# Token layout and a masked multiply for the first chunk's four attention tiles

## The chip, the core and the metric

The kernel runs on one core of one Trainium2 chip. The metric is device time in microseconds (us), the median of several runs. The engines work side by side, each through its own queue in order: PE (TensorE: matmuls and transposes, results in PSUM), DVE (VectorE) and ACT (ScalarE), which do elementwise work, POOL (GpSimd), which does elementwise work on SBUF alone, and SP (SyncE), which only issues transfers here.

## What is computed

A linear attention with a decaying state over 768 tokens (4 batches, 8 heads of 48 channels), then two feed-forward blocks on its 3072 token rows of 384 channels. The attention, cut to what the change touches:

```
for t in range(S):
    cur = einsum('bhd,bhe->bhde', u * k[t], v[t])
    y[t] = einsum('bhd,bhde->bhe', r[t], state + cur)
    state = w[t][..., None] * state + einsum('bhd,bhe->bhde', k[t], v[t])
x = y.transpose(0, 2, 1, 3).reshape(B * S, H * D)
h = x @ moe_w_in;  g = h * clip(h + 3, 0, 6) / 6;  x = g @ moe_w_out
```

The second block (`moe2`) comes after that and is not touched.

## The kernel before

**Tiles and stages.** The tokens are cut into 6 chunks of 128; with 4 batches that makes 24 tiles, tile i being chunk i // 4 of batch i % 4. The attention of a tile goes through six stages. `stw` clips the decay w (`wc`, L403). `st0` transposes w and r on PE (`wt`, `rt`, L397), and DVE runs a cumulative product over the tokens from each side (`q` at L427, `e` at L433, in four instructions each) and scales r by it (L437). `st1` transposes k (`kt`), DVE scales it (`q`, L452), and POOL forms z = r * k * u (L454, L455). `st2` transposes the scaled k back to tokens (`ktp`, copied to `ktok` by ACT) and forms the products of all keys and queries: `pa0` for the even and `pa1` for the odd heads (L477), 128 x 4 x 128 each. DVE sums z to a diagonal d (L473); POOL writes ident * d into `am` (L483), and DVE copies pa over it where the causal mask is set (L487). `st3` computes the state update `kv` (L497), copied into `s_st` by DVE (L523), and the output `yt` (L511) with **channels on the partitions**: v is the weight (48 columns) and `am` the moving operand (128 columns). ACT copies it out (`ys`, L527), two transfers write it to `x1d` in DRAM (L528), and one reads it back as `xf`, with 384 channels as three groups of 128 partitions (L530). `st4` splits it into a high part `xh` (ACT, L546) and a low part `xl` (POOL, L547).

**The first feed-forward block** runs in slots: `ffn_in(n)` is nine matmuls over `xh` and `xl` with the high and low parts of the weights (`h`, L565), then ACT, DVE, ACT and DVE or POOL (`t`, `gh`, `gl`, L569 to L573); `ffn_out(n)` follows two slots later (`y`, L585). One chunk (four tiles) takes 16 slots. It starts when `xh` and `xl` of tiles 0 to 3 are there.

**The weights** of the first block come as 64-bit floats in 16 blocks and are decoded on the way: per block four DVE steps on 128x768 (L40, L43, L50, L53), an ACT copy for the high part (`w_h`, L60) and a POOL subtraction for the low part (`w_l`, L61). Blocks 0 to 3 are begun ahead of the slots, the others at one per slot.

**What sets the order.** Ahead of the slots, a table of ticks calls the stages of tiles 0 to 3 (`starts` and `decodes`, L677 to L690). In it SP and POOL keep the order in which the code issues their work, while a scheduler orders PE, DVE and ACT. Attention tiles share three PSUM buffers (`ps_tile`, L391), so a stage's PE work waits until an earlier tile's PSUM has been read. From tile 4 on the scheduler spreads the stages over the slots.

Of the kernel before, what the change touches and what calls it, by code (L numbers as in the profile page):

```python
# [8 lines left out]
F32 = mybir.dt.float32  # L9
# [3 lines left out]
ACTF = mybir.ActivationFunctionType  # L13
# [5 lines left out]
P = 128  # L19
# [248 lines left out]
def fast_path(  # L268
# [189 lines left out]
    def st2(i):  # L458
        a = at[i]
        g = i // B  # L460
        kq = a["q"][:, :, 1:C + 1]
        rr = a["e"]
        if g < NG - 1:
            ktp = ps_tile("ktp")
            for hp in range(HP):
                nc.tensor.transpose(out=ktp[:, hp, 0:DP], in_=kq[0:DP, hp, :], identity=ident[0:DP, 0:DP])
            ktok = atp.tile([P, HP, DP], F32, tag="ktok", name="ktok")
            nc.scalar.activation(out=ktok, in_=ktp[:, :, 0:DP], func=ACTF.Copy)
            a["ktok"] = ktok
        a["am"] = []  # L470
        pas = [ps_tile("pa0"), ps_tile("pa1")]
        d = atp.tile([P, H], F32, tag="d", name="d")
        nc.vector.tensor_reduce(out=d, in_=a["z"], axis=AX.X, op=ALU.add)  # L473
        heads = [(j, hh) for j in range(HP) for hh in range(2)]
        for j, hh in heads:
            pa, o = pas[hh], 64 * hh
            nc.tensor.matmul(  # L477
                out=pa[:, j, :], lhsT=kq[o:o + D, j, :], rhs=rr[o:o + D, j, :], start=True, stop=True
            )
        dv = d.rearrange("p (j hh) -> p hh j", hh=2)  # L480
        for hh, pa in enumerate(pas):
            am = atp.tile([P, 4, C], F32, tag="am", name="am")
            nc.gpsimd.tensor_tensor(  # L483
                out=am, in0=ident.unsqueeze(1).to_broadcast([P, HP, C]),
                in1=dv[:, hh, :].unsqueeze(2).to_broadcast([P, HP, C]), op=ALU.mult,
            )
            nc.vector.copy_predicated(am, causal.unsqueeze(1).to_broadcast([P, HP, C]), pa)  # L487
            a["am"].append(am)

    def st3(i):  # L490
        a = at[i]
        g, b = divmod(i, B)
        vv = a["v"].rearrange("p h d -> p (h d)")
        if g < NG - 1:
            kv = ps_tile("kv")
            for hp in range(HP):
                nc.tensor.matmul(  # L497
                    out=kv[0:DP, hp, 0:2 * D], lhsT=a["ktok"][:, hp, :], rhs=vv[:, hp * 2 * D:(hp + 1) * 2 * D],
                    start=True, stop=True,
                )  # L500
        y = ps_tile("yt")
        for hp in range(HP):
            for j in range(2):
                if g > 0:
                    nc.tensor.matmul(  # L505
                        out=y[64 * j:64 * j + D, hp, :], lhsT=a["sp"][0:DP, hp, j * D:(j + 1) * D],
                        rhs=a["e"][0:DP, hp, :], start=True, stop=False,
                    )
            for j in range(2):
                h = 2 * hp + j  # L510
                nc.tensor.matmul(  # L511
                    out=y[64 * j:64 * j + D, hp, :], lhsT=vv[:, h * D:(h + 1) * D], rhs=a["am"][j][:, hp, :],
                    start=(g == 0), stop=True,
                )
        if g < NG - 1:
            for j in range(2):
                o, f = 64 * j, D * j
                dst = s_st[b][o:o + D, :, f:f + D]
                src = kv[o:o + D, :, f:f + D]
                if g > 0:  # L520
                    nc.vector.tensor_tensor(out=dst, in0=src, in1=a["sp"][o:o + D, :, f:f + D], op=ALU.add)
                else:
                    nc.vector.tensor_copy(out=dst, in_=src)  # L523
        ys = atp.tile([P, HP, C], F32, tag="ys", name="ys", bufs=1)
        for j in range(2):
            o = 64 * j
            nc.scalar.activation(out=ys[o:o + D], in_=y[o:o + D], func=ACTF.Copy)  # L527
            nc.sync.dma_start(out=x1d[i, :, j].rearrange("h d t -> d h t"), in_=ys[o:o + D])  # L528
        xf = atp.tile([P, KD, C], F32, tag="xf", name="xf")
        nc.sync.dma_start(  # L530
            out=xf, in_=x1d[i].rearrange("h j d t -> (h j d) t").rearrange("(c p) t -> p c t", p=P)
        )
        a["xf"] = xf

    def st4(i):
        a = at.pop(i)
        g, b = divmod(i, B)
        if b == 0:
            x_t[g] = (
                xp.tile([P, KD, GT], F32R, tag="xh", name="xh"),  # L540
                xp.tile([P, KD, GT], F32R, tag="xl", name="xl"),
            )
        xh, xl = x_t[g]
        xf = a["xf"]
        sl = slice(b * C, (b + 1) * C)
        nc.scalar.activation(out=xh[:, :, sl], in_=xf, func=ACTF.Copy, accum_out=chk[:, 3 * i + 2:3 * i + 3])  # L546
        nc.gpsimd.tensor_tensor(out=xl[:, :, sl], in0=xf, in1=xh[:, :, sl].bitcast(F32), op=ALU.subtract)  # L547

    stages = [stw, st0, st1, st2, st3, st4]

# [293 lines left out]
```

## Time and profile before

| what | us |
|---|---|
| median of 3 runs (845.01 to 847.47) | 845.86 |
| the profiled execution's own time | 846.06 |
| span of its records, first to last instruction | 844.3 |
| busy in that span: PE / DVE / ACT / POOL | 784.8 / 537.1 / 350.9 / 289.6 |

The program has three parts that can be told apart in the page's slices of 21 us: up to about 84 us the attention of the first four tiles (PE 5 and 4 tenths busy in the first two slices), then the first feed-forward block until somewhat after 600 us, with the decoding of its weights up to about 174 us, and the second block behind it. A busy share is to be read by part: a mean over the span says nothing of which engine sets the pace in one of them.

### The profile page before, as it was taken

To read this page: it belongs to the slowest core of one execution; us is meant where nothing else is said; L and a number is where in the kernel's file an instruction comes from. 1 tells how busy PE (TensorE), PEld (TensorE's weight loads), DVE (VectorE), ACT (ScalarE), POOL (GpSimd) and SP (SyncE) were. 2 spreads that over 40 slices of the span, in tenths; PEclk is the share of its full clock that TensorE was granted. 3 is DMA by queue.
4 is the path that set the end of the run, shared out by engine and by line. 5 is a ranking of instruction groups with operands and counts; after the bars stand their busy time and mean duration, and the time that the engine had idled before them with its cause. 6 is when DMAs were issued, how large, how long until landed. Compare 5 with 4: busy or idle time off the path is not lost.

```text
span 844.3 us, 12276 instructions
## 1 busy us (share of the span) xinstructions
PE 784.8 (93%) x4546; PEld 661.8 (78%) x4546; DVE 537.1 (64%) x992; ACT 350.9 (42%) x655; POOL 289.6 (34%) x383
## 2 busy tenths in 40 slices
PE   5486988799999999999999999998999999999995
PEld 4364766588888888888888888786789999999995
DVE  5876999975656555555666665689564555555451
ACT  2342545444333434443444333455353443444341
POOL 4276567554333332233333321133122222222210
PEclk9766998899999999999999999999999999999998
DMA  9758354524222322232222200443011111111101
GB/s 189 138 85 205 103 181 110 121 57 123 66 57 56 85 48 57 53 83 53 57 48 52 76 19 19 115 126 113 0 66 47 39 47 48 38 47 37 39 19 34
DMA packets 149382, 62.45 MB, mean 74 GB/s; under 512 B 103872, under 2 KB 143936, under 8 KB 149312
## 3 DMA queue, kind: packets, MB, share of 16 engines
q1 hardware_dynamic: 146720, 56.84, 27.9%
q10 hardware_dynamic: 2592, 4.72, 1.5%
q8 instruction: 38, 0.62, 0.3%
q14 instruction: 32, 0.26, 0.1%
HBM read 47.39 MB, written 14.16 MB: 73 GB/s over the span
## 4 chain that ended last, share of the span: by engine, by line
PE 74%; DVE 13%; issue 5%; DMA 2%; ACT 2%; POOL 2%; SPq 1%; POOLq 0%; ACTq 0%; DVEq 0%
PE y L585 18%; PE h L565 17%; PE po L780 12%; PE h L753 12%; DVE dec L50 3%; PE pa L477 3%; PE yt L511 3%; PE pt L767 2%; PE yt L505 2%; DVE dec L53 2%; PE kv L497 2%; DVE raw L43 1%; DVE dec L40 1%; DVE t L570 1%; PE wt L397 1%
## 5 line engine op out<-in xcount | busy, mean ns | idle before, releaser
L569 ACT ACTIVATE t<-h,three 128x512 f32<-128x512 f32 x96 | 65.7, 684 | 134.7 <-PE h L565 134.4
L585 PE MATMUL y<-gh,w_h 128*128 128x512 f32 x288 | 121.0, 420 | 0.0
L565 PE MATMUL h<-xh,w_h 128*128 128x512 f32 x288 | 114.3, 397 | 5.5 <-DVE t L570 5.5
L565 PE MATMUL h<-xl,w_h 128*128 128x512 f32 x288 | 113.3, 393 | 3.7 <-POOL xl L547 3.7
L585 PE MATMUL y<-gh,w_l 128*128 128x512 f32 x288 | 113.5, 394 | 0.0
L565 PE MATMUL h<-xh,w_l 128*128 128x512 f32 x288 | 113.4, 394 | 0.0
L585 PE MATMUL y<-gl,w_h 128*128 128x512 f32 x288 | 113.3, 394 | 0.0
L571 ACT ACTIVATE gh<-t 128x512 fp32r<-128x512 f32 x96 | 60.5, 630 | 85.9 <-DVE t L570 85.7
L570 DVE SCALAR_TENSOR_TENSOR t<-t,h 128x512 f32<-128x512 f32 x96 | 65.4, 681 | 45.1 <-ACT t L569 45.1
L483 POOL TENSOR_TENSOR am<-ident,d 128x512 f32<-128x512 f32 x48 | 54.3, 1149 | 109.7 <-PE yt L511 109.5
L573 DVE TENSOR_TENSOR gl<-t,gh 128x512 fp32r<-128x512 f32 x88 | 71.7, 815 | 29.3 <-ACT gh L571 27.8
L427 DVE TENSOR_TENSOR_SCAN q<-wt,ones 112x128 f32<-112x128 f32 x96 | 34.5, 407 | 69.2 <-PE wt L397 69.2
L565 PEld LDWEIGHTS h<-xh,w_h 128*128 128x128 f32 x288 | 54.7, 190 | 19.7 <-DVE t L570 8.5
L67 DVE TENSOR_REDUCE nm<-h 128x1 f32<-128x1024 f32 x24 | 29.4, 1225 | 62.5 <-PE h L753 62.5
L780 PE MATMUL po<-w_oh,qh 128*128 128x384 f32 x192 | 67.0, 349 | 0.3 <-ACT qh L769 0.3
L565 PEld LDWEIGHTS h<-xl,w_h 128*128 128x128 f32 x288 | 54.7, 190 | 15.7 <-POOL xl L547 4.5
L585 PEld LDWEIGHTS y<-gh,w_h 128*128 128x128 f32 x288 | 54.6, 190 | 15.5 <-issue 4.0
L780 PE MATMUL po<-w_oh,ql 128*128 128x384 f32 x192 | 65.2, 339 | 0.1
L780 PE MATMUL po<-w_ol,qh 128*128 128x384 f32 x192 | 65.0, 339 | 0.0
L585 PEld LDWEIGHTS y<-gh,w_l 128*128 128x128 f32 x288 | 54.5, 189 | 12.2
L565 PEld LDWEIGHTS h<-xh,w_l 128*128 128x128 f32 x288 | 54.6, 190 | 11.6
L585 PEld LDWEIGHTS y<-gl,w_h 128*128 128x128 f32 x288 | 54.9, 190 | 9.8 <-DVE gl L573 0.3
(104 smaller groups left out, 1616.1 us busy)
## 6 DMA issues: line engine op xcount, KB each, us to landing
raw<-in_moe_w_in_dram SPq DMA_DIRECT2D x24, 384.0 KB, 3.7
raw<-in_moe_w_out_dram SPq DMA_DIRECT2D x24, 384.0 KB, 4.2
w<-in_w_dram SPq DMA_DIRECT2D x24, 192.0 KB, 3.3
r<-in_r_dram SPq DMA_DIRECT2D x24, 192.0 KB, 3.3
k<-in_k_dram SPq DMA_DIRECT2D x24, 192.0 KB, 3.9
v<-in_v_dram SPq DMA_DIRECT2D x24, 192.0 KB, 3.0
x1d<-ys SPq DMA_DIRECT2D x48, 96.0 KB, 2.3
xf<-x1d SPq DMA_DIRECT2D x24, 192.0 KB, 2.7
```

What stands on the lines that cost most here:

```text
L50: nc.vector.scalar_tensor_tensor(out=f, in0=f, scalar=3, in1=raw[:, :, 1], op0=ALU.logical_shift_left, op1=ALU.bitwise_or)
L67: nc.vector.tensor_reduce(out=nm, in_=h, axis=AX.X, op=ALU.max, negate=True)
L427: nc.vector.tensor_tensor_scan(out=q[0:DP, hp, 0:C][:, ::-1], data0=wt[0:DP, hp, :][:, ::-1], data1=ones[0:DP, :], initial=1.0, op0=ALU.mu ...
L483: nc.gpsimd.tensor_tensor(out=am, in0=ident.unsqueeze(1).to_broadcast([P, HP, C]), in1=dv[:, hh, :].unsqueeze(2).to_broadcast([P, HP, C]), ...
L565: nc.tensor.matmul(out=h, lhsT=a, rhs=b, start=(j == 0), stop=(j == len(ops) - 1))
L569: nc.scalar.activation(out=t, in_=h, func=ACTF.Relu, bias=three)
L570: nc.vector.scalar_tensor_tensor(out=t, in0=t, scalar=6.0, in1=h, op0=ALU.min, op1=ALU.mult)
L571: nc.scalar.activation(out=gh, in_=t, func=ACTF.Copy)
L573: eng.tensor_tensor(out=gl, in0=t, in1=gh.bitcast(F32), op=ALU.subtract)
L585: nc.tensor.matmul(out=y_ps[g][c], lhsT=a, rhs=b, start=(m == 0 and j == 0), stop=(m == M1 - 1 and j == 2))
L753: nc.tensor.matmul(out=h[:, fs], lhsT=a[:, c, :], rhs=b_[:, c, fs], start=(j == 0), stop=(j == len(ops) - 1))
L780: nc.tensor.matmul(out=po, lhsT=x[:, m, :], rhs=y[:, m, :], start=(n == 0), stop=(n == 3 * M2 - 1))
```

## The change

For tiles 0 to 3 (`first`, g == 0), which have no earlier state to add:

- The products of the even heads are computed ahead of those of the odd ones. ACT copies `pa0` to `am`, and POOL masks it in place (`affine_select`, 128x512); DVE multiplies `pa1` with the mask. No diagonal is written into `am`: d * v is computed on POOL (`av`, 128x384).
- The output matmul has `am` as its weight (128 columns) and v as its moving operand (48 columns), so that **tokens** lie on the partitions. DVE adds `av` while it takes the result out of PSUM (`ys`, 128x384).
- No transfer through `x1d`: three PE transposes put `ys` into PSUM (`px`), ACT takes `xh` from there, and DVE, no longer POOL, forms `xl`.

```diff
@@ st2
+        if first:
+            heads.sort(key=lambda x: x[1])
...
+            if first:
+                if hh == 0:
+                    nc.scalar.activation(out=am, in_=pa, func=ACTF.Copy)
+                    nc.gpsimd.affine_select(
+                        out=am, in_=am, pattern=[[0, 4], [1, P]], compare_op=ALU.is_gt, fill=0.0, base=0,
+                        channel_multiplier=-1,
+                    )
+                else:
+                    mask = causal.bitcast(F32).unsqueeze(1).to_broadcast([P, 4, C])
+                    nc.vector.tensor_tensor(out=am, in0=pa, in1=mask, op=ALU.mult)
+                continue
...
+        if first:
+            d = atp.tile([P, H], F32, tag="d", name="d")
+            nc.vector.tensor_reduce(out=d, in_=a["z"], axis=AX.X, op=ALU.add)
+            av = atp.tile([P, H, D], F32, tag="xf", name="av")
+            nc.gpsimd.tensor_tensor(out=av, in0=a["v"], in1=d.unsqueeze(2).to_broadcast([P, H, D]), op=ALU.mult)
+            a["av"] = av
@@ st3
+            if g == 0:
+                for j in range(2):
+                    h = 2 * hp + j
+                    nc.tensor.matmul(
+                        out=yf[:, h * D:(h + 1) * D], lhsT=a["am"][j][:, hp, :], rhs=vv[:, h * D:(h + 1) * D],
+                        start=True, stop=True,
+                    )
+                continue
...
+        if g == 0:
+            ys = ys.rearrange("p h t -> p (h t)")[:, 0:DM]
+            nc.vector.tensor_tensor(out=ys, in0=yf, in1=a["av"].rearrange("p h d -> p (h d)"), op=ALU.add)
+            a["ys"] = ys
+            return
@@ st4
+        if g == 0:
+            xf = ps_tile("px")[:, 0:KD, :]
+            for c in range(KD):
+                nc.tensor.transpose(out=xf[:, c, :], in_=a["ys"][:, c * P:(c + 1) * P], identity=ident)
+            eng = nc.vector
+        else:
+            xf, eng = a["xf"], nc.gpsimd
...
-        nc.gpsimd.tensor_tensor(out=xl[:, :, sl], in0=xf, in1=xh[:, :, sl].bitcast(F32), op=ALU.subtract)
+        eng.tensor_tensor(out=xl[:, :, sl], in0=xf, in1=xh[:, :, sl].bitcast(F32), op=ALU.subtract)
```

The scheduler and the queues answer with another order. Three places of it follow; line numbers are those of each kernel. First **SP**, from the load of tile 3's k onward. In the kernel before:

```order
L381 DMA k<-in_k_dram 128x8x48
L388 DMA v<-in_v_dram 128x8x48
L528 DMA x1d<-ys 48x4x128 x2
L530 DMA xf<-x1d 128x3x128
L31 DMA raw<-in_moe_w_in_dram 128x3x256
L31 DMA raw<-in_moe_w_out_dram 128x768
L381 DMA w<-in_w_dram 128x8x48
```

and in the changed kernel:

```order
L381 DMA k<-in_k_dram 128x8x48
L388 DMA v<-in_v_dram 128x8x48
L31 DMA raw<-in_moe_w_in_dram 128x3x256
L31 DMA raw<-in_moe_w_out_dram 128x768
L381 DMA w<-in_w_dram 128x8x48
L381 DMA r<-in_r_dram 128x8x48
```

The write to `x1d` and the read back, which stood ahead of the loads for weight block 2 and tile 4, are gone from there; so they are for tiles 1 to 3.

Second **POOL**, where the first weight block's low part meets tile 1 (`w1_l` is that low part). Before:

```order
L455 TENSOR_TENSOR z_301<-z_301,u_bc_98 128x384
L425 MEMSET q_314 112x4
L61 TENSOR_TENSOR w1_l_115<-dec_332,w1_h_114 128x768
L547 TENSOR_TENSOR xl_348<-xf_293,xh_347 128x3x128
L483 TENSOR_TENSOR am_370<-ident_62,d_360 128x512
L483 TENSOR_TENSOR am_373<-ident_62,d_360 128x512
```

and changed:

```order
L455 TENSOR_TENSOR z_297<-z_297,u_bc_98 128x384
L425 MEMSET q_310 112x4
L61 TENSOR_TENSOR w1_l_115<-dec_328,w1_h_114 128x768
L490 AFFINE_SELECT am_368<-am_368 128x512
L508 TENSOR_TENSOR av_375<-v_159,d_373 128x384
```

Tile 0's `xl`, which stood between the weight's low part and tile 1's `am`, is on DVE now; the mask and `av` stand there.

Third **PE**, from the last of the four tiles to the first feed-forward matmul. Before, tile 4's whole attention comes ahead of the first `h` (some twenty rows further down); its beginning:

```order
L497 MATMUL kv<-v,ktok 112x96 x4
L511 MATMUL yt<-am,v 48x128
L397 MATMUL wt<-ident,wc 112x128 x4
L511 MATMUL yt<-am,v 48x128 x7
L397 MATMUL rt<-ident,r 112x128 x4
L397 MATMUL kt<-ident,k 112x128 x4
L466 MATMUL ktp<-ident,q 128x112 x4
```

Changed:

```order
L518 MATMUL kv<-v,ktok 112x96 x4
L528 MATMUL yt<-v,am 128x48 x8
L583 MATMUL px<-ident,ys 128x128 x3
L397 MATMUL wt<-ident,wc 112x128 x4
L397 MATMUL rt<-ident,r 112x128 x4
L606 MATMUL h<-xh,w_h 128x512 x2
L397 MATMUL kt<-ident,k 112x128 x4
```

The first `h` stands right behind the first transposes of tile 4, and the rest of that tile's attention is spread between the `h` matmuls behind it. Further down the two orders meet again: from the fourteenth slot of the first chunk on they are equal on every engine, row for row.

## Rows read from the trace of the kernel before

**Rows 1.** Windows: us, busy us (instructions) of PE, PEld, DVE, ACT, POOL; PEclk, DMA, GB/s

```profile
22.60:38.40 15.80, 5.56 (x36) 4.38 (x36) 15.38 (x31) 6.10 (x13) 2.52 (x2) 0.73 0.87 155
52.00:62.00 10.00, 8.33 (x46) 6.90 (x46) 5.04 (x12) 5.49 (x14) 6.30 (x7) 0.50 0.55 81
...
59.50:83.10 23.60, 15.34 (x103) 11.84 (x102) 15.78 (x34) 6.80 (x15) 16.37 (x22) 0.64 0.71 182
...
60.60:85.30 24.70, 16.44 (x103) 12.92 (x103) 17.98 (x35) 6.85 (x16) 16.98 (x21) 0.64 0.69 175
84.00:174.00 90.00, 76.90 (x429) 61.41 (x429) 84.68 (x105) 44.20 (x76) 56.19 (x44) 0.90 0.46 121
180.00:600.00 420.00, 415.58 (x2523) 342.50 (x2522) 265.49 (x490) 175.26 (x334) 130.82 (x166) 1.00 0.27 68
```

**Rows 2.** Timeline, tile 0's way back: start us, us, instruction [idle before <-releaser]

```profile
23.39 1.58 SPq L528 DMA_DIRECT2D x1d<-ys  x2
...
27.39 0.38 SPq L530 DMA_DIRECT2D xf<-x1d  x1
...
37.44 0.51 ACT L546 ACTIVATE xh<-xf 128x384 fp32r<-128x384 f32 x1
38.12 1.00 POOL L547 TENSOR_TENSOR xl<-xf,xh 128x384 fp32r<-128x384 f32 x1 [4.40 <-ACT xh L546]
38.49 1.07 PE L397 MATMUL rt<-ident,r 128*112 128x128 f32 x4 [5.74 <-issue]
39.07 2.04 POOL L483 TENSOR_TENSOR am<-ident,d 128x512 f32<-128x512 f32 x2
```

**Rows 3.** Timeline, the last tile's low part and the first feed-forward matmul waiting for it

```profile
81.97 3.25 DVE L40 TENSOR_SCALAR dec<-raw 128x768 f32<-128x768 f32 x1 [2.06 <-POOL w_l L61]
82.04 0.99 POOL L547 TENSOR_TENSOR xl<-xf,xh 128x384 fp32r<-128x384 f32 x1
82.99 1.82 POOL L61 TENSOR_TENSOR w_l<-dec,w_h 128x768 fp32r<-128x768 f32 x1
83.09 0.79 PE L565 MATMUL h<-xl,w_h 128*128 128x512 f32 x1 [3.74 <-POOL xl L547]
```

**Rows 4.** Groups by line, shapes apart: xcount | busy us, mean ns | idle before

```profile
L569 ACT ACTIVATE t<-h,three 128x512 f32<-128x512 f32 x96 | 65.7, 684 | 134.7 <-PE h L565 134.4
...
L454 POOL TENSOR_TENSOR z<-r,k 128x384 f32<-128x384 f32 x24 | 28.2, 1175 | 41.6 <-DMA k<-in_k_dram 26.8 <-issue 13.8 <-POOL k L380 0.7
...
L452 DVE TENSOR_TENSOR q<-kt,q 112x512 f32<-112x512 f32 x24 | 16.3, 680 | 0.8 <-PE kt L397 0.8
...
L329 POOL TENSOR_SCALAR_AFFINE_SELECT causal<-ones 128x128 f32<-128x128 f32 x1 | 0.3, 294 | 0.0
```

**Rows 5.** Timeline of DVE: decode steps, a scan and the state's copies

```profile
32.16 2.37 DVE L50 SCALAR_TENSOR_TENSOR dec<-dec,raw 128x768 int32<-128x768 int32 x1
...
35.73 0.93 DVE L53 SCALAR_TENSOR_TENSOR dec<-raw,dec 128x768 int32<-128x768 int32 x1
...
36.78 1.60 DVE L433 TENSOR_TENSOR_SCAN e<-wt,e,ones 112x127 f32<-112x127 f32 x4
...
43.66 0.71 DVE L523 COPY s_st<-kv 48x192 f32<-48x192 f32 x2
...
105.16 0.55 DVE L40 TENSOR_SCALAR dec<-raw 128x768 f32<-128x768 f32 x1
```

**Rows 6.** Timeline of PE and its weight loads (PEld) in the four tiles

```profile
19.49 1.55 PEld L511 LDWEIGHTS yt<-am,v 128*48 128x48 f32 x16 [1.22 <-PE kv L497]
...
23.35 0.60 PE L397 MATMUL rt<-ident,r 128*112 128x128 f32 x4
...
52.47 3.09 PE L477 MATMUL pa<-e,q 48*128 48x128 f32 x16
...
55.49 1.57 PEld L497 LDWEIGHTS kv<-v,ktok 128*112 128x112 f32 x8 [0.23 <-issue]
55.49 1.81 PE L497 MATMUL kv<-v,ktok 128*112 128x96 f32 x8
```

**Rows 7.** Timeline of ACT, the start of each tile's copy out, tiles 1 to 3

```profile
43.91 1.21 ACT L527 ACTIVATE ys<-yt 48x512 f32<-48x512 f32 x2 [5.27 <-PE yt L511]
...
51.69 1.21 ACT L527 ACTIVATE ys<-yt 48x512 f32<-48x512 f32 x2 [4.68 <-PE yt L511]
...
62.54 1.21 ACT L527 ACTIVATE ys<-yt 48x512 f32<-48x512 f32 x2 [4.75 <-PE yt L511]
```

More of the change, by code (lines that the diff above doesn't have):

```diff
@@ L471, in st2 @@
         pas = [ps_tile("pa0"), ps_tile("pa1")]
-        d = atp.tile([P, H], F32, tag="d", name="d")
-        nc.vector.tensor_reduce(out=d, in_=a["z"], axis=AX.X, op=ALU.add)
+        first = i < B
+        if not first:
+            d = atp.tile([P, H], F32, tag="d", name="d")
+            nc.vector.tensor_reduce(out=d, in_=a["z"], axis=AX.X, op=ALU.add)
         heads = [(j, hh) for j in range(HP) for hh in range(2)]
+        if first:
+            heads.sort(key=lambda x: x[1])
         for j, hh in heads:
@@ L479, in st2 @@
             )
-        dv = d.rearrange("p (j hh) -> p hh j", hh=2)
         for hh, pa in enumerate(pas):
             am = atp.tile([P, 4, C], F32, tag="am", name="am")
+            a["am"].append(am)
+            if first:
[9 more added lines that the diff above has]
+                continue
+            dv = d.rearrange("p (j hh) -> p hh j", hh=2)
             nc.gpsimd.tensor_tensor(
@@ L487, in st2 @@
             nc.vector.copy_predicated(am, causal.unsqueeze(1).to_broadcast([P, HP, C]), pa)
-            a["am"].append(am)
+        if first:
+            d = atp.tile([P, H], F32, tag="d", name="d")
+            nc.vector.tensor_reduce(out=d, in_=a["z"], axis=AX.X, op=ALU.add)
+            av = atp.tile([P, H, D], F32, tag="xf", name="av")
+            nc.gpsimd.tensor_tensor(out=av, in0=a["v"], in1=d.unsqueeze(2).to_broadcast([P, H, D]), op=ALU.mult)
+            a["av"] = av
     def st3(i):
@@ L501, in st3 @@
         y = ps_tile("yt")
+        yf = y.rearrange("p h t -> p (h t)")[:, 0:DM]
         for hp in range(HP):
+            if g == 0:
[6 more added lines that the diff above has]
+                continue
             for j in range(2):
@@ L543, in st4 @@
         xh, xl = x_t[g]
-        xf = a["xf"]
         sl = slice(b * C, (b + 1) * C)
+        if g == 0:
[5 more added lines that the diff above has]
+            xf, eng = a["xf"], nc.gpsimd
         nc.scalar.activation(out=xh[:, :, sl], in_=xf, func=ACTF.Copy, accum_out=chk[:, 3 * i + 2:3 * i + 3])
-        nc.gpsimd.tensor_tensor(out=xl[:, :, sl], in0=xf, in1=xh[:, :, sl].bitcast(F32), op=ALU.subtract)
+        eng.tensor_tensor(out=xl[:, :, sl], in0=xf, in1=xh[:, :, sl].bitcast(F32), op=ALU.subtract)
     stages = [stw, st0, st1, st2, st3, st4]
```

## The prediction

> **What bounds the kernel now.** I read the windows first, since a share of the whole span mixes parts with different limits. From 180 to 600 us PE is busy 415.6 of 420 us [rows 1]: there nothing but less PE work would help, and the change does not touch it. From 84 to 174 us it is DVE, with 84.7 of 90 us, while PE has 76.9 [rows 1]; DVE decodes twelve weight blocks there beside its other work. Ahead of 84 us no engine is full: from 60.6 to 85.3 us DVE is busy 18.0 of 24.7 us and PE 16.4 [rows 1]. That part is bound by waits. Two of them can be named in the timeline. Tile 0's x goes to DRAM at 23.39 us, is read back from 27.39 us, is split by ACT at 37.44 us and reaches POOL at 38.12 us, ahead of tile 1's `am` at 39.07 us; PE starts its next transposes at 38.49 us after 5.74 us of idling [rows 2]. At the end the first feed-forward matmul on `xl` waits 3.74 us, until 83.09 us, for POOL to form the last low part at 82.04 us [rows 3].
>
> Since DVE is full behind 84 us, an early start of the feed-forward block is worth only what DVE gains by it: the time in which DVE neither idles nor is held up. As the two orders are equal from slot 14 on, a lead of DVE by then is a lead of the whole program, PE having slack until there. So I follow DVE from a common place to a common place. The place in the kernel before is 60.6 us, where DVE has finished tiles 0 to 3 and weight blocks 0 to 2, and 85.3 us, where tile 4, half of tile 5, block 3 and the first step of block 4 are done as well.
>
> **The change, part by part.** *Removed transfers:* eight writes and four reads leave SP. No engine waits for them directly in the walk below, so I count nothing for them alone; their worth lies in the order that they allow.
>
> *The first tile.* The products of even and odd heads no longer alternate; a row of another tile with the two kinds apart takes 3.09 us [rows 6], and this delays nothing by itself except `kv`, by 0.15 us. The output matmul now loads 128 columns as weights instead of 48. Today's sixteen loads take 1.55 us; eight loads of 112 columns take 1.57 us, or 0.196 each [rows 6]. Sixteen at that price are 3.1 us; I take 3.2, with 1.6 (no dearer) and 3.6 (in proportion to columns, 128/112) as ends. The trace thus shows wider loads to be dearer. The Trainium skill, "TensorE: Matmul & The Clock Gate", section on LDWEIGHTS, says the same against this change: a load costs its columns over 1.2 in ns, whatever the rows; by it sixteen loads rise by 16 x 80 / 1.2 ns = 1.07 us a tile (an estimate), a little less than the 1.65 us taken here, and the sum would be about 1.5 us better.
>
> With `yt` from 19.65 to 22.85 us and DVE's add behind it (0.55 us, between three quarters of the 0.68 us for 512 elements and the whole of it [rows 4]) the next scaling of k begins at 23.4 us, where it stands near 22.6 us before. So far the change loses 0.8 us.
>
> *From there to the end of the scans of tile 3.* In the kernel before this is the window from 22.6 to 38.4 us, 15.38 us of DVE work [rows 1]. Of it, two steps of weight block 1 (2.37 and 0.93 us [rows 5]) come later in the new order; `xl` of tile 0 (0.55), the mask of tile 1 (0.68 [rows 4]) and the state's copies (0.71 [rows 5]) come earlier. That is 15.38 - 3.30 + 1.94 = 14.0 us. I add 0.5 us for `kv` (1.81 us of PE, of which a scan covers most [rows 6]) and 2.0 us for a decode step held up by POOL's `w_l`. That holding up is seen twice: L50 took 2.37 us where L53, of the same size, took 0.93, and L40 took 3.25 us, until POOL's `xl` and `w_l` were over, instead of 0.55 [rows 3, 5]; I take the middle of 1.4 and 2.7. The scans end at 23.4 + 16.5 = 39.9 us. `yt` of tile 1 began when the state's copies were done, 1.8 us before (a reciprocal and the scans of 1.60 us [rows 5]), so DVE waits 1.4 us and then adds: 41.9 us.
>
> *Tiles 2 and 3* follow in a loop in which PE is the longest part: `pa` 3.09, `kv` 1.81, `yt` 3.2 and eleven transposes for `ktp`, `kt` and `px` at 1.07 us for four [rows 2, 6], 11.0 us in all. The granted clock in such a stretch is 0.50, the lower of the two levels [rows 1]; but the same four transposes also took 0.60 us [rows 6], at which rate the loop takes 6.2 us. I take the middle, 8.6 us. The kernel before needed 7.8 and 10.9 us from one tile's `ys` to the next [rows 7], so this is near what hand-overs allow. ACT's copy of `pa0` (0.68 us [rows 4]) and POOL's mask (four times 0.294 us, 1.2 us; 0.3 if the size does not count [rows 4]) lie beside `pa1`, `kt`, `px` and `kv` on PE, 5.4 us at the lower level; `av` (1.2 us at most [rows 4]) is needed only by the add. These cost nothing as long as together they stay below that; without the cover the sum pays 1.9 us a tile. Two loops end at 59.1 us; three transposes (0.64), ACT's `xh` (0.51 [rows 2], 0.7 with its hand-overs) and DVE's `xl` (0.55) end at 61.0 us.
>
> *What follows.* DVE now stands where it stood at 60.6 us before: the four tiles alone give nothing, as a heavier PE loop eats what the round trip gave back. The gain lies in the next stretch. Before, DVE needed 24.7 us for 17.98 us of work, of which 2.70 us is L40 held up [rows 1, 3, 5]: 15.3 us of its own. In the new order that work is spread beside the first `h` matmuls, and neither `xl` on POOL nor tile 5's transposes stand in its way. I leave 1.0 us of idling (0 to 3) and 2.5 us for decode steps held up by POOL (0 to 5.4, twice the worst seen). So the common place is reached at 61.0 + 15.3 + 3.5 = 79.8 us instead of 85.3 us: 5.5 us gained, and 846.06 - 5.5 = **840.6 us** in the profiled execution's own time, which is 0.2 us above the median of the three runs.
>
> The twelve new DVE steps read one operand from PSUM, as L452 does, whose 24 have a mean of 0.68 us [rows 4], the price taken here, so I add no holding up for them. The Trainium skill, "SBUF — State Buffer", section "Who interferes with whom", says so too: DVE and POOL exclude each other when DVE has two SBUF inputs or runs in a mode with two ports, and not otherwise. By that rule only the decode steps pay. If the new steps could be held up like L50, by 1.4 us each, 17 us would be at stake; no row shows that.
>
> *The ends.* The loop at 6.2 or 11.0 us moves the sum by 4.8 us either way, holding up by 4.5 us down or 0.9 up, idling by 1 down or 2 up. Not all fall on one side; 834.5 to 845.5 us is the likeliest case's own range.
>
> **The rivals.** *PE sets the pace behind 61 us.* If DVE has more slack than I give it, what counts is PE's account: the block's first matmuls run 83.1 - 61.0 = 22.1 us earlier, and PE work of tiles 4 and 5 moves behind them: 15.3 us were busy from 59.5 to 83.1 us [rows 1], less some 1.55 for tile 3's `yt` and 2 x 0.79 for two early `h` [rows 3, 6], 12.2 us. The gain is 9.9 us: 836.2 us. Against it: DVE's 84.7 of 90 us. For it: the moved work is priced at the lower clock level, and would shrink where PE is dense.
>
> *The lead is given back.* If PE stays at the lower level through the loop (11.0 us), the gain shrinks by 4.8 us to 845.4 us, within what can be told from no change. For it: a granted clock of 0.50 from 52 to 62 us [rows 1]. Against it: PE idles less in the new order.
>
> *Slower.* The new path makes PE's next step depend on a chain of five hand-overs per tile: `yt` to DVE's `ys`, to `px`, to `xh`, to `xl`, and with three PSUM buffers PE waits for one of these to be read. If that adds 2 us to a loop at the lower level (13 us), 2 x 4.4 us are lost against my sum, 8.8 us, and 846.06 + 3.3 = 849.4 us comes out. It decides from a loop of 11.35 us on, where the gain is gone. For it: 10.9 us were seen for one loop [rows 7] with fewer PE hand-overs. Against: between `px` and the next tile there is other PE work.
>
> That the change does not do what it says is excluded: the transfers are gone from the order of SP.
>
> **How the numbers follow.** A measurement of this kernel tells about 0.3% (2.5 us) from no change. Forecast (834.5 to 843.3 us): 0.54. PE's account: 0.15. Lead given back: 0.19. Slower: 0.12. So faster 0.69, same 0.19, slower 0.12. The range for 8 in 10 reaches from 833.5 us (half of PE's account beyond it) to 847.5 us (most of the slower case beyond it).
>
> **What would show it.** In the changed kernel: `ys` of tiles 1 to 3 near 41, 50 and 59 us, the first `h` near 61 us, the first step of block 4 near 80 us, the last step of block 15 some 5 us earlier than now, and behind it the same PE part with the same length. Wrong would be: loops of 6 or of 13 us between the tiles, DVE with much more idling than 1 us between 61 and 80 us, decode steps of blocks 3 and later longer than now, or a PE part that changes its length.

## The result, and the profile after

The changed kernel took 835.46 us (median of 4 runs, 834.57 to 838.21), the kernel before 846.08 us in the same session: a ratio of 0.988, interval 0.985 to 0.991, so 10.6 us faster. The forecast was 840.6 us with 833.5 to 847.5 us as its range: right direction, inside the range, half of the gain missed. The span fell from 844.3 to 832.4 us.

Windows of the changed kernel; the columns are those of [rows 1] (us, then busy us of PE, PEld, DVE, ACT and POOL, then the granted clock):

```profile
40.00:60.00 20.00, 19.28 (x98) 18.39 (x97) 11.52 (x21) 5.73 (x14) 9.97 (x15) 0.50 0.41 92
61.25:67.96 6.71, 6.71 (x29) 5.43 (x27) 6.71 (x15) 2.98 (x8) 6.63 (x8) 0.72 0.70 174
67.96:161.99 94.03, 78.22 (x463) 62.69 (x463) 93.28 (x127) 46.00 (x79) 65.87 (x54) 0.87 0.48 133
170.00:590.00 420.00, 415.68 (x2521) 342.34 (x2520) 265.83 (x489) 175.03 (x334) 130.74 (x166) 1.00 0.27 67
```

and, cut at the same places of the work, two windows of the kernel before:

```profile
60.60:87.62 27.02, 18.76 (x109) 14.66 (x109) 19.93 (x37) 8.34 (x17) 16.98 (x21) 0.63 0.63 161
87.62:172.98 85.36, 72.26 (x417) 57.95 (x415) 81.43 (x101) 41.68 (x72) 55.33 (x42) 0.92 0.48 127
```

The places are: the end of DVE's work for the four tiles (60.6 us before, where POOL's last `xl` is still to come; 61.25 us after, with the last `xl`), DVE's first `t`, and the end of the last decode step of block 15 (172.98 and 161.99 us). DVE reaches the first place 0.65 us later than before. The first `t` comes 19.7 us earlier, since tile 4 and half of tile 5 no longer stand ahead of it; that work is done behind it, so the stretch from there is 8.7 us longer. What remains is 11.0 us, and it can be booked: DVE's busy time over both windows fell by 1.4 us (101.36 to 99.99), its idle time by 10.2 us (11.0 to 0.75), less the 0.65 us of the later start. The PE part behind it is as long as it was: 415.68 busy of 420 us, as in the last row of [rows 1].

The timeline of DVE after gives the steps that the prediction named (start, us, instruction, idle before it and what released it): the four `ys`, the last `xl` and the first and the fourteenth `t`:

```profile
21.00 0.54 DVE L557 TENSOR_TENSOR ys<-yt,av 128x384 f32<-128x384 f32 x1
...
38.82 0.56 DVE L557 TENSOR_TENSOR ys<-yt,av 128x384 f32<-128x384 f32 x1 [2.25 <-PE yt L528]
...
49.03 0.56 DVE L557 TENSOR_TENSOR ys<-yt,av 128x384 f32<-128x384 f32 x1 [1.62 <-PE yt L528]
...
58.53 0.56 DVE L557 TENSOR_TENSOR ys<-yt,av 128x384 f32<-128x384 f32 x1 [2.64 <-PE yt L528]
...
60.69 0.56 DVE L588 TENSOR_TENSOR xl<-px,xh 128x384 fp32r<-128x384 f32 x1 [0.28 <-ACT xh L587]
...
67.96 0.66 DVE L611 SCALAR_TENSOR_TENSOR t<-t,h 128x512 f32<-128x512 f32 x1
...
163.48 0.69 DVE L611 SCALAR_TENSOR_TENSOR t<-t,h 128x512 f32<-128x512 f32 x1 [1.22 <-ACT t L610]
```

In the kernel before, the first and the fourteenth `t` start at 87.62 and 174.47 us. Where [rows 3] showed PE waiting 3.74 us for the last low part, `ys` to `xl` now takes 2.7 us; before, it took 20.5 us from the start of ACT's copy of tile 3 at 62.54 us [rows 7] to the end of POOL's `xl` at 83.03 us [rows 3].

### The profile page after: what moved, and what is told of

It reads as the page before. It is cut to its first block, busy times and chain, and to the rows that moved or that the text cites. A ratio compares the mean times of both kernels' runs of the same rounds, so it can differ in the third digit from the quotient of the medians.

```text
span 832.4 us, 12272 instructions
## 1 busy us (share of the span) xinstructions
PE 792.3 (95%) x4558; PEld 673.5 (81%) x4558; DVE 534.0 (64%) x996; ACT 348.6 (42%) x651; POOL 285.7 (34%) x379
## 4 chain that ended last, share of the span: by engine, by line
PE 78%; DVE 14%; issue 4%; ACT 2%; DMA 1%; SPq 0%; POOL 0%; ACTq 0%; DVEq 0%; POOLq 0%
PE y L626 19%; PE h L606 17%; PE po L821 12%; PE h L794 12%; PE pa L481 4%; DVE dec L50 3%; PE pt L808 2%; PE yt L535 2%; PE kv L518 2%; DVE raw L43 2%; PE yt L541 2%; DVE dec L53 2%; DVE dec L40 2%; PE yt L528 1%; DVE t L611 1%
## 5 line engine op out<-in xcount | busy, mean ns | idle before, releaser
L499 POOL TENSOR_TENSOR am<-ident,d 128x512 f32<-128x512 f32 x40 | 45.1, 1147 | 110.5 <-PE yt L541 104.5
```

Of the source, the lines that this page charges most:

```text
L499: nc.gpsimd.tensor_tensor(out=am, in0=ident.unsqueeze(1).to_broadcast([P, HP, C]), in1=dv[:, hh, :].unsqueeze(2).to_broadcast([P, HP, C]), ...
```

## The experiments

All times below are medians; the ratio is to the kernel before in the same session (845.65 to 846.55 us). "First t" and "14th t" are the starts of these DVE steps in the profiled execution, in us. From the fourteenth `t` on the order of work is the same in the kernel before and in the changed one; in all kernels here the span ends 667 to 673 us after it, so a lead there carries to the end to within some 3 us.

A mark of one execution laid beside a mark of another is less exact than a median. The changed kernel, x1 and x12 issue the same instructions in the same order on every engine until the last `xl`, and yet it comes 58.33 us after the start in x1, 60.69 us in the changed kernel and 62.62 us in x12; the lines of x1 and x12:

```profile
58.33 0.56 DVE L588 TENSOR_TENSOR xl<-px,xh 128x384 fp32r<-128x384 f32 x1 [0.28 <-ACT xh L587]
62.62 0.56 DVE L588 TENSOR_TENSOR xl<-px,xh 128x384 fp32r<-128x384 f32 x1 [0.28 <-ACT xh L587]
```

Part of it is `yt` of tile 0, which took 1.96 us in x1 and the changed kernel and 3.62 us in x12 (also in x4 and x5). So differences of marks below some 4 us prove nothing by themselves. And of x4 the profiled execution (837.13 us) was 3.1 us shorter than the median, of x12 (846.09 us) 3.9 us longer.

| kernel | median us | ratio | first t | 14th t |
|---|---|---|---|---|
| before | 846.1 | 1 | 87.62 | 174.47 |
| changed | 835.5 | 0.988 | 67.96 | 163.48 |
| x3 before, no round trip (stand-in) | 835.9 | 0.988 | 71.20 | 165.96 |
| x8 before, xl on DVE | 843.7 | 0.998 | 87.31 | 171.60 |
| x4 changed, old mask | 840.3 | 0.993 | 70.94 | 167.28 |
| x10 before, heads sorted | 844.8 | 0.998 | 87.74 | 174.05 |
| x6 changed, heads alternating | 826.4 | 0.977 | 62.59 | 155.64 |
| x11 x6 with the mask on DVE alone | 825.5 | 0.976 | 59.33 | 154.11 |
| x5 changed, a block decoded earlier | 842.7 | 0.994 | 73.38 | 169.49 |
| x7 x6, a block decoded earlier | 839.0 | 0.991 | 67.69 | 165.05 |
| x9 x6, a block decoded later | 826.7 | 0.976 | 62.52 | 157.53 |
| x1 changed, more DVE work | 845.6 | 0.999 | 65.60 | 172.87 |
| x2 before, more DVE work | 848.5 | 1.003 | 85.69 | 172.87 |
| x12 changed, more PE work | 842.2 | 0.996 | 69.88 | 173.12 |

**Which part brings the gain: x3, x8, x4.** x3 takes the transfers out of the kernel before and puts only a copy from PSUM in their place (and POOL clears the tile first):

```diff
+        if g == 0:
+            xf = atp.tile([P, KD, C], F32, tag="xf", name="xf")
+            nc.gpsimd.memset(xf, 1.0)
+            for j in range(2):
+                o = 64 * j
+                nc.scalar.activation(out=xf[o:o + D], in_=y[o:o + D, 0:KD], func=ACTF.Copy)
+            a["xf"] = xf
+            return
```

> The kernel before, channel layout and old mask kept, but for tiles 0 to 3 xh and xl are taken from an SBUF copy of the output itself (384 elements on 128 partitions as before, in a wrong arrangement of channels; POOL clears the tile first), so the write to DRAM and the read back are gone and nothing takes their place: the rearrangement is left out. If the round trip is all that the change removes of value, this comes to the time of the changed kernel or better: 831 to 837 us. If token layout, mask and xl on DVE carry a part (POOL still stands between w_l, xl and am here), only some of the gain shows: 838 to 843 us. If the lead of the four tiles is worthless because DVE is full behind them: 844 to 847 us.

Measured: ratio 0.988 (0.986 to 0.990), 835.9 us. Without the round trip the old layout and the old mask reach the time of the changed kernel. Whether the price lies in POOL's place alone is told by x8, which moves only `xl`:

```diff
-        nc.gpsimd.tensor_tensor(
+        (nc.vector if g == 0 else nc.gpsimd).tensor_tensor(
             out=xl[:, :, sl], in0=xf, in1=xh[:, :, sl].bitcast(F32), op=ALU.subtract)
```

> The kernel before with xl of tiles 0 to 3 formed by DVE and no longer by POOL; the round trip through DRAM, the mask and the layout stay. If what the round trip costs is that POOL, in its order, waits for it ahead of tile 1's am (38.12 us in the kernel before), this alone brings most of that back: 837 to 841 us. If the latency of the transfers itself is on the path, at tile 3's end above all, only the 1 to 2 us of POOL's subtraction at the end go: 843.5 to 845.5 us.

Measured: 0.998 (0.996 to 0.999), 843.7 us: 2 to 3 us, the second reading. In its trace POOL's `am` of tile 1 does start earlier (33.95 instead of 39.07 us), but the first `h` on `xl` still comes at 83.61 us. The timeline of SP in the kernel before shows how the last two tiles' x goes out and back; the columns are start, us, instruction:

```profile
52.30 1.08 SPq L528 DMA_DIRECT2D x1d<-ys  x2
53.48 0.41 SPq L388 DMA_DIRECT2D v<-in_v_dram  x1
63.60 0.39 SPq L381 DMA_DIRECT2D r<-in_r_dram  x1
64.10 0.52 SPq L530 DMA_DIRECT2D xf<-x1d  x1
...
65.78 0.86 SPq L528 DMA_DIRECT2D x1d<-ys  x2
...
70.96 0.37 SPq L530 DMA_DIRECT2D xf<-x1d  x1
```

and SP's waits there (what waited for whom, us in total, times, longest):

```profile
SPq L381 <- PE rt L397: 9.7, 1, 9.7
```

Tile 2's output is written at 52.30 us and read back only at 64.10 us, since a load of `r` stands in front of the read and waits 9.7 us for PE to release its buffer. Tile 3's write, for a copy begun at 62.54 us [rows 7], is issued at 65.78 us, its read at 70.96 us. The wait of 9.7 us itself is not on the path to the first `h` on `xl`, which needs all four tiles: tile 2's `xl` is done at 69.17 us, tile 3's at 83.03 us. Tile 3's write only comes 2.0 us late by it (its copy ends at 63.75 us). What holds tile 3's x after its read are the orders of ACT and POOL; two lines of ACT and one of POOL:

```profile
76.02 0.84 ACT L60 ACTIVATE w_h<-dec 128x768 fp32r<-128x768 f32 x1 [0.73 <-DVE dec L53]
...
77.37 0.51 ACT L546 ACTIVATE xh<-xf 128x384 fp32r<-128x384 f32 x1
```

```profile
80.13 1.80 POOL L61 TENSOR_TENSOR w_l<-dec,w_h 128x768 fp32r<-128x768 f32 x1
```

The reads of the first tiles land 2.6 to 3.6 us after their issue, so tile 3's x is there at some 73.6 to 74.6 us; ACT takes it 3 to 4 us later, behind tile 4's `ys` and the weights' `w_h`, and POOL forms `xl` at 82.04 us [rows 3], behind tile 4's `am` and z and the weights' `w_l`. Of the 20.5 us some 11 to 12 go with ACT's copy, the transfers and their places on SP, the rest with the places of `xh` and `xl` behind other work. In x8, where `xl` is off POOL, ACT takes `xh` only at 80.67 us. So x3 removes the time of the transfers and, with it, the late places of `xh` and `xl` on ACT and POOL; how the 10 us divide between the two was not told apart.

x4 keeps the new layout and the sorted heads and puts the old mask back: in `st2` all tiles take the way of the later ones, with ident * d on POOL and the copy under the mask on DVE, and

```diff
-            nc.vector.tensor_tensor(out=ys, in0=yf, in1=a["av"].rearrange("p h d -> p (h d)"), op=ALU.add)
+            nc.vector.tensor_copy(out=ys, in_=yf)
```

> The changed kernel with the old mask in tiles 0 to 3: POOL writes ident times d into am, DVE copies pa over it under the mask, and the output is copied out of PSUM without an addition. Layout, transposes and xl on DVE stay. If the masked multiply has a part in the gain (one DVE step of 0.7 us per tile less, and am no longer behind POOL's w_l), 838 to 842 us; if the layout alone carries it, 834 to 837 us.

Measured: 0.993 (0.991 to 0.995), 840.3 us, 4.8 us slower than the changed kernel. Its last `xl` ends at 65.26 us, 4.0 us later than in the changed kernel, and DVE's window from there to the end of block 15 is

```profile
65.26:165.79 100.53, 86.03 (x504) 69.44 (x504) 99.83 (x140) 48.78 (x83) 72.71 (x61) 0.88 0.50 134
```

as long as in the changed kernel (100.74 us), with as little idling (0.70 us). Of the 4.0 us, 1.7 stand at tile 0's `ys` already (22.70 against 21.00 us), where `yt` took 3.62 us as in x12, so the trace doesn't tell what the mask alone costs there; 3.8 us are left at the fourteenth `t`, and 2.6 us between the two profiled executions (837.13 and 834.57 us). One thing follows: the small idle time behind 61 us does not come from an early start, since a later start keeps it; it goes with the new order, which leaves tile 4's and 5's work to be done between the slots' steps. Put together: taking the round trip out is worth 10 us; what comes in its place, transposes, wider weights and sorted heads, costs about 4.4 us of them (x4 against x3); the new mask gives 4.8 us back (changed kernel against x4; their intervals, 0.985 to 0.991 and 0.991 to 0.995, lie side by side). The parts don't add up beyond that: undoing the sorting alone, which is next, gains more than the 4.4 us.

**What the sorted heads cost: x6, x10, x11.** x6 undoes the sorting in the changed kernel:

```diff
-        if first:
-            heads.sort(key=lambda x: x[1])
```

> The changed kernel with the products of even and odd heads alternating again in tiles 0 to 3 (no sorting); nothing else. Eight products in a row of one kind apart take 3.09 us in the changed kernel at the lower clock level. If PE's loop is what sets the end of the four tiles, and alternating products are shorter as in the later tiles of the kernel before, the loop loses 0.5 to 1 us each and the first feed-forward matmul comes 2 to 4 us earlier: 831.5 to 833.5 us. If ACT's copy and POOL's mask of pa0 need the cover of the second half, they come onto the path and cost as much: 834.5 to 838 us.

Measured: 0.977 (0.975 to 0.978), 826.4 us: 9 us faster than the changed kernel, and far more than expected. PE in the loops of tiles 2 and 3, first the changed kernel:

```profile
39.43 3.09 PE L481 MATMUL pa<-e,q 48*128 48x128 f32 x16
...
45.45 3.54 PE L528 MATMUL yt<-v,am 128*128 128x48 f32 x16
...
49.70 3.09 PE L481 MATMUL pa<-e,q 48*128 48x128 f32 x16
...
54.88 3.54 PE L528 MATMUL yt<-v,am 128*128 128x48 f32 x16
```

then x6:

```profile
38.33 2.67 PE L479 MATMUL pa<-e,q 48*128 48x128 f32 x16
...
43.70 1.91 PE L526 MATMUL yt<-v,am 128*128 128x48 f32 x16
...
45.95 1.54 PE L479 MATMUL pa<-e,q 48*128 48x128 f32 x16
...
50.77 3.62 PE L526 MATMUL yt<-v,am 128*128 128x48 f32 x16 [1.71 <-DVE am L494]
```

and its window, to be laid beside the first row of the changed kernel's windows above:

```profile
40.00:60.00 20.00, 17.51 (x104) 16.05 (x103) 15.22 (x29) 8.92 (x21) 13.13 (x19) 0.67 0.59 133
```

With the two kinds apart, PE is busy 19.28 of 20 us and the granted clock stays at the lower level (0.50); with the two kinds alternating, PE is busy 17.51 us and the granted clock is 0.67: it is 1.00 over tile 2's `yt` and tile 3's `pa` (1.91 and 1.54 us) and 0.50 over the other two lines. So the shorter products and the clock are mixed in these lines, and that the first brought the second was not shown: in x4, with the heads sorted, the granted clock is 0.67 there as well. At the same clock the order alone is seen in tile 0, where the products take 2.08 against 3.09 us (lines at the end) and `ys` comes 1.1 us earlier (19.93 against 21.00 us). The last `xl` ends at 57.22 instead of 61.25 us, the fourteenth `t` comes 7.8 us earlier. So 4.0 us are won in the four tiles; 3.8 us more come behind them, where DVE ends block 15 after 96.9 instead of 100.7 us: a decode step is done ahead, and the 51 left take 55.9 us, where the 52 of the changed kernel took 59.7. The scheduler answers the edit with another order of DVE, ACT, POOL and SP from tile 2 on, and why the steps are held up less was not told apart.

The same sorting in the kernel before is x10:

```diff
+        if i < B:
+            heads.sort(key=lambda x: x[1])
```

> The kernel before with the products of the even heads ahead of those of the odd ones in tiles 0 to 3, as the changed kernel has them; nothing else. If the order of the heads delays next to nothing by itself, as the prediction had it: 844.5 to 847.5 us. If it makes PE's loop longer and holds PE at its lower clock level, as the gain of 9 us from undoing it in the changed kernel suggests, 849 to 855 us here, or somewhat less where the loop before waits on the round trip anyway.

Measured: 0.998 (0.997 to 0.999), 844.8 us: no cost, if anything 1 us of gain. PE has slack there, 16.63 of 20 us busy from 40 to 60 us. But the edit does little in that kernel. `pa` of tiles 0 and 2 in the kernel before:

```profile
11.59 2.08 PE L477 MATMUL pa<-e,q 48*128 48x128 f32 x16
...
44.52 1.80 PE L477 MATMUL pa<-e,q 48*128 48x128 f32 x16 [0.15 <-DVE s_st L523]
```

and of tiles 0, 2 and 3 in x10:

```profile
11.42 3.09 PE L479 MATMUL pa<-e,q 48*128 48x128 f32 x16
...
44.00 1.74 PE L479 MATMUL pa<-e,q 48*128 48x128 f32 x16
...
52.59 3.09 PE L479 MATMUL pa<-e,q 48*128 48x128 f32 x16
```

Tile 3 takes 3.09 us in the kernel before as well [rows 6]: though the code alternates the heads, the scheduler's order had the two kinds largely apart in tiles 1 to 3 already, and the sorting changes tile 0 alone by much. So x10 shows that 1 us more of PE work in tile 0 costs nothing there; what products apart cost the later tiles of the kernel before, no run shows.

x11 gives both halves of the mask to DVE in x6 (`if hh == 0:` becomes `if False:`, so that ACT's copy and POOL's `affine_select` go).

> The kernel x6 (826.4 us) with both halves of the mask multiplied by DVE: ACT's copy of pa0 (0.60 us) and POOL's mask (0.64 us) of each of the four tiles go, and one DVE step of 0.69 us comes in. If ACT and POOL were beside the path, DVE pays 0.7 us a tile at most where it waits for PE: 826 to 829 us. If the POOL half is what the output's matmul waits for: 822 to 825.5 us.

Measured: 0.976 (0.973 to 0.978), 825.5 us. In its trace the four tiles end 3.6 us earlier than in x6 (`xl` done at 53.61 us) and the fourteenth `t` comes 1.5 us earlier; the time is 1 us shorter, within its interval, which reaches into both readings. Whether a lead is given back behind, or belongs to that one execution, was not told apart.

**Where the four tiles hand over: x5, x7, x9.** DVE idles 12 us between 21.6 and 61.2 us in the changed kernel. x5 puts a weight block there:

```diff
-    LD = 3
+    LD = 4
...
-    decodes = {4: [0, 1], 7: [2], 9: [3]}
+    decodes = {4: [0, 1], 6: [2], 8: [3], 9: [4]}
```

> The changed kernel with one more weight block decoded ahead of the slots (block 3 whole and the first half of block 4; each later block one slot earlier). DVE idles 12 us between 21.6 and 61.2 us in the changed kernel while PE sets the pace there, and has 0.75 us of idling behind. If DVE's work behind 61 us sets the time, one block of four decode steps (4.6 us with the time held up, 3.8 without) leaves it and hides ahead: 830.5 to 832.5 us. If the steps come in the way of the scans and of ys, or POOL's low part in the way of z, the first matmul on x comes as much later as DVE is relieved: 834 to 838 us.

Measured: 0.994 (0.993 to 0.996), 842.7 us, 7 us slower, where the first reading had 4 us of gain and the second at most 838 us. x7 is the same edit on x6:

> The changed kernel with both: one block decoded earlier, heads alternating. If DVE sets the time behind and PE the end of the four tiles, the two gains add up: 827 to 831 us. If PE becomes the bound behind 61 us when DVE is relieved (PE idles 15 us there in the changed kernel, some of it at hand-overs), the second brings nothing: as the better of the two alone.

Measured: 0.991 (0.990 to 0.993), 839.0 us, 12.6 us slower than x6, outside both readings. My reading, that any DVE work taken from behind 61 us is won, fell. The table suggests why: in x7 the first `t` comes 5.1 us later than in x6, since the steps of another block now stand ahead of it, and each slot still decodes one block. Only one slot at the end has no block to decode, and at that end (160 to 180 us) PE is busy 20.00 of 20 us in x5, x6 and x7 alike, so that DVE's relief is worth nothing. What seems to count is when the slots' `t` come, not when the decoding ends: x12 below finishes block 15 at 157.32 us, 4.7 us ahead of the changed kernel, and is slower. (x5's `ys` of tile 0 is late by 1.8 us already, ahead of any step that moved, since `yt` took 3.62 us there; so the pair x6 and x7 is the cleaner one.)

If so, decoding later should gain. x9 starts from x6:

```diff
-    LD = 3
+    LD = 2
...
-    decodes = {4: [0, 1], 7: [2], 9: [3]}
+    decodes = {4: [0, 1], 7: [2]}
```

> The kernel x6 (changed kernel with heads alternating, 826.4 us) with one weight block fewer decoded ahead of the slots: block 3 is begun in slot 0, each later block one slot later. If what counts is how early DVE reaches the first t, and the decoding's end is covered by PE's dense part (as the two kernels with one block more, 7 to 12 us slower, suggest), the reverse gains: the first t 3 to 5 us earlier, 820 to 824 us. If DVE's total work behind the four tiles counts, it loses a block of 4 us: 829 to 832 us. If the weights now come too late for h: slower than 832 us.

Measured: 0.976 (0.974 to 0.979), 826.7 us, as x6, in none of the three ranges. The first `t` didn't come earlier (62.52 against 62.59 us), and PE now waits for the weights (what waited for whom, us in total, times, longest, from 57 to 170 us):

```profile
PE h L604 <- POOL w_l L61: 7.2, 6, 2.5
PE ktp L466 <- DVE q L452: 4.1, 1, 4.1
```

Of two, three and four blocks ahead, two and three are equal and four is worse.

**Which engine sets the pace behind 61 us: x1, x2, x12.** x1 and x2 add 24 DVE steps to slots 0 to 11 (first diff), x12 adds 48 matmuls in `ffn_in` (second diff):

```diff
+        if n < 12:
+            for x in range(2):
+                nc.vector.tensor_reduce(
+                    out=ones[:, 0:4], in_=ones[:, 4:P].unsqueeze(1).to_broadcast([P, 4, P - 4]), axis=AX.X, op=ALU.max
+                )
```

```diff
+        if n < 12:
+            ops = ops[:1] * 4 + ops
```

> The changed kernel with two more DVE steps in each of slots 0 to 11 (reductions of 496 elements over constants, 24 in all, whose result nobody uses; as L473 before took 0.535 us for 384 elements, some 0.55 to 0.65 us each, 13 to 15 us together). If DVE sets the pace from 61 to 162 us (0.75 us idle there), nearly all of it comes out: 10 to 15 us longer, 845 to 851 us. If PE's account is what counts (PE is idle 15 of these 101 us and takes on nothing), 0 to 3 us: 835 to 838 us.

> The kernel before with the same 24 DVE steps. DVE idles 4.3 us in slots 0 to 14 and 6.7 us ahead of them. If DVE is the bound there too, and its idle time is only where it has run ahead of PE, ACT and POOL, the steps fill some of it: 8 to 13 us longer, 854 to 859 us, some 1 to 4 us less than the same steps cost in the changed kernel. If PE or the round trip sets the pace in before, under 4 us: 846 to 850 us.

> The changed kernel with four more matmuls of 128 x 512 in each of slots 0 to 11 (the first product of h added four times more, 48 in all, so h of these slots is not the reference's). At some 0.23 us from one to the next, as in the dense part of the changed kernel, they are 11 us of PE work. If DVE sets the pace from 61 to 162 us, where PE idles 15 us, they vanish in the gaps: 0 to 4 us longer, 835.5 to 839.5 us. If PE's account is what counts: 8 to 11 us longer, 843.5 to 847 us.

The price of the added steps, as a group, here of x1 (mean ns of one behind the busy us); in x2 it is the same, 15.8 us and 658 ns:

```profile
L754 DVE TENSOR_REDUCE ones<-ones 128x4 f32<-128x496 f32 x24 | 15.8, 658 | 0.0
```

Of 15.8 us, the changed kernel pays some 10 us (845.6 us; ratio 0.999, 0.997 to 1.001), the kernel before only 2.8 us (848.5 us; 1.003, 1.002 to 1.004). Of some 11 us of matmuls the changed kernel pays 6.7 us (842.2 us; 0.996, 0.994 to 0.997), between the two expectations. These shares are rough, as the ten executions of x1 lie between 841.4 and 850.3 us and those of x12 between 840.2 and 846.1 us: in x1's trace, whose four tiles end 2.4 us earlier, the stretch from there to the end of block 15 is 13.3 us longer than in the changed kernel. Still, each engine's added work comes out for the larger part, and neither engine's account holds alone. The waits say how the two are coupled. PE in the changed kernel, 61.25 to 162 us:

```profile
PE ktp L466 <- DVE q L452: 14.6, 3, 6.4
PE h L606 <- DVE t L611: 0.8, 2, 0.5
PE h L606 <- POOL w_l L61: 0.4, 1, 0.4
```

and DVE in x12, 63 to 175 us (the longest only):

```profile
DVE t L613 <- ACT t L612: 5.5, 3, 3.5
```

Nearly all of PE's 15.8 us of idling are three waits for DVE's scaled k, once per tile, and DVE has that step late because it is full in between. But matmuls added elsewhere hardly fall into these three gaps, which still come to 11.9 us in x12: they delay `h`, DVE waits 5.5 us for its `t`, and the scaled k is later with it. In the same way x1's added steps put DVE out of step with POOL (7.3 us of waits for `am`). For the kernel before, x2 shows that its DVE was not the bound between 84 and 174 us although it was busy 94% of it: the four decode steps of a block, 59.5 us in all there, took 52.8 us in x2, because less of them was held up, and other DVE work moved behind block 15, where DVE has room.

## Why the prediction was right, and where it was not

**The four tiles: the sum was right by two errors.** 61.0 us was forecast for the last `xl`, 61.25 us measured. On the way, `ys` came at 21.00 (its end and the next scaling of k were put at 23.4 us, `yt` at 3.2 us; it took 1.96 us at a granted clock of 0.99, the upper level), 38.82 (forecast 41), 49.03 (50) and 58.53 us (59). The 2.0 us for a decode step held up there were not paid: L43 of block 1 took 0.55 us. Against that, `yt` of tile 1 took 3.62 us and DVE waited 2.25 us for it, where 1.4 had been put. Tile 1's `ys` thus ended 2.5 us ahead of the forecast, and the loop took them back: 10.2 and 9.5 us where 8.6 us had been taken, the middle between both levels of the clock, and PE stayed at the lower one (0.50). `yt` in the loop took 3.54 us, at the upper of its ends. That they cancelled is luck, and so is the 1.96 us: in x12, whose order is the same, `yt` of tile 0 took 3.62 us. The price of the wider weights is to be read at one clock level. With 48 columns, in x10 (tile 2, granted clock 0.50) and in x3 (tile 3, 1.00):

```profile
49.77 1.95 PE L513 MATMUL yt<-am,v 128*48 128x128 f32 x16
```

```profile
56.54 1.51 PE L511 MATMUL yt<-am,v 128*48 128x128 f32 x16
```

So 128 columns cost some 1.6 us a tile at the lower level (3.54 against 1.95 us), as much as the 1.65 us of the prediction, and some 0.4 us at the upper one (1.91 us in x6, tile 2, against 1.51). The 1.07 us a tile of the Trainium skill's rule, from "TensorE: Matmul & The Clock Gate", section on LDWEIGHTS, lie between the two; with them the sum would have been some 2 us better, and not 1.5, as the chain has four `yt`.

**The sorted heads: the step was wrong.** The sorting "delays nothing by itself except `kv`, by 0.15 us", said the prediction. In the changed kernel it costs 9 us (x6), and `kv` of tile 0 comes 1.1 us later by it (16.33 against 15.23 us). x10 agrees with the sentence for tile 0 of the kernel before, and there alone. The 3.09 us stood in the sum of the loop, but not as a price of the change to be set against the 2.08 us that alternating products take before, and what more PE work does to the clock was not asked.

**The removed transfers: counted at nothing by themselves, worth the whole gain.** x3 shows it: with the transfers alone out, and nothing of the new layout, the time is that of the changed kernel. The prediction gave them a worth only through the order that they allow, 5.5 us in all. It followed tile 0's round trip to its end and priced POOL's `xl` at tile 3's, but took the twenty microseconds between tile 3's copy and its `xl` as time in which DVE has 15.3 us to do in any case. The rows of SP, ACT and POOL that show what stands ahead of tile 3's x were not read. Nor was ACT's row in tile 0's round trip: from the read's issue at 27.39 us [rows 2] to ACT's `xh` at 37.44 us it is not the transfer that lasts, which lands within 3.6 us, but ACT's order. `w_h` of a weight block stands ahead of `xh` and waits 4.56 us for DVE's decoding:

```profile
36.69 0.84 ACT L60 ACTIVATE w_h<-dec 128x768 fp32r<-128x768 f32 x1 [4.56 <-DVE dec L53]
```

**What follows, the term mis-sized.** 24.7 us of DVE between the two places were to become 18.8 us, of which 3.5 us for idling and hold-ups: with the later start, a gain of 5.5 us, next to all of it idle time (6.7 us to 1.0). The idle time that went was 10.2 us, 7.1 of it ahead of the first `t` and 3.2 behind it, in the stretch that the prediction took as full and unchanged (84.7 of 90 us). A stretch with 5.3 us of idling and with decode steps that stretch by collision was not full; x2 shows that it had room for most of 15.8 us. The marker named for it, the first step of block 4 near 80 us, was badly chosen: it came at 70.00 us, with tile 4's work behind it. That the lead at slot 14 is the program's lead was right, to within 3 us for all kernels here.

**No holding up of the new steps: right.** The mask's multiply took 0.688 us (mean of 4), `ys` 0.554, `xl` 0.552 us, with POOL busy beside them. The decode steps were held up as before, 59.7 us for 52 steps against 59.5 us, with single ones at 3.92 us (L53 at 83.42 us). The rule of the Trainium skill that the prediction took ("SBUF — State Buffer", section "Who interferes with whom") is in agreement with both. (The cover of 5.4 us for ACT's copy and POOL's mask adds up to 5.2; the two took 0.60 and 0.64 us, far below it.)

**The rivals.** PE's account gave 836.2 us, next to the result, but its mechanism alone is not it: PE still idles 15.8 us, nearly all of it for DVE's steps, x12 passes on about 6.7 of 11 us of added PE work, and x1 some 10 of 15.8 us of added DVE work. That the number fits is luck. The slower case asked for loops of 11.35 us, and one came to 10.2 us; the lead given back asked for 11.0 us. Both were near in the loops, and neither came about, since far more was gained behind the four tiles than the sum had there.

## What to carry to other kernels

Work out what a transfer in the middle of a chain costs from the queue that issues it: the row to read is what stands in front of it there and what that waits for. Then do the same for the engine that takes the data and the next one: here the places of `xh` and `xl` behind other work cost tile 3 some 8 us after its data had landed. A busy share of 94% is no proof of a bound when some of the busy time is instructions stretched by another engine; add work and see how much of it comes out. And when a change moves the bound to another engine, price every edit again for that engine: here undoing one line of the change nearly doubled its gain (826.4 us, 2.3% under the kernel before). Before a line is called free elsewhere, look whether it changed the order there at all.

## What was not expected of the hardware

The sixteen matmuls of `pa`, two for each head, take 2.08 us with rows 0 to 47 and 64 to 111 alternating and 3.09 us with the two kinds apart, at the same place of the program, tile 0; first x6, then the changed kernel:

```profile
11.47 2.08 PE L479 MATMUL pa<-e,q 48*128 48x128 f32 x16
```

```profile
11.55 3.09 PE L481 MATMUL pa<-e,q 48*128 48x128 f32 x16
```

The profile's windows give 1.00 as the granted clock there, but its records of the clock begin only at 16.1 and 17.2 us, and the durations are those of the lower level: four transposes take 1.01 us at 10.6 us and 0.58 us at 25.14 us, where 1.00 is recorded, and products apart take the same 3.09 us in the loop at 0.50. At a recorded 1.00 the pair is 1.16 us, for a later tile of the kernel before with the kinds alternating, and 1.74 us, in x10's tile 2 with the kinds largely apart (its line is above):

```profile
187.41 1.16 PE L477 MATMUL pa<-e,q 48*128 48x128 f32 x16
```

So at either level apart is longer by half. The Trainium skill, "TensorE: Matmul & The Clock Gate", section "Why this matters for your kernels", says that products with few rows run side by side where they lie in different row groups of the array. These runs agree, and the rule speaks against sorting them, which the prediction didn't weigh.

PE at 96% busy, from 40 to 60 us, was granted the lower level (0.50) throughout, while at 88% in x6 it was granted 0.67. A busy share is itself larger at the lower level, where the same work takes longer (`yt` 3.54 us, against 1.91 us in x6 at 1.00), so it doesn't tell how much PE has to do.

POOL's `affine_select` took 0.635 us for 128x512 in place (mean of 4), against 0.294 us for 128x128 [rows 4], where the prediction had 1.2 us, in proportion, as its upper bound.
